# A planned attention and gMLP kernel: PSUM lent between two uses, score blocks of three, the product of the g rows moved, and a new order of tasks

## The chip, the cores and the metric

The kernel runs on one core of one Trainium2 chip. The metric is the time of one execution on the device, in microseconds (us). A core has four engines that matter here, each with its own instruction queue: TensorE (PE, the matrix multiplier; its weight loads are listed apart as PEld), ScalarE (ACT), VectorE (DVE) and GpSimd (POOL). SyncE (SP) issues transfers. Matrix products land in PSUM, which has 8 banks; one bank holds 512 float32 numbers in each of 128 partitions, and only ACT and DVE read it out here.

## The reference

Batch B = 8, heads H = 12, sequence S = 448, head width D = 64. Everything the kernel takes and gives is float32.

```python
def rmsnorm(x, g):
    return x / np.sqrt(np.mean(x * x, axis=-1, keepdims=True) + 1e-06) * g
q_n, k_n = rmsnorm(q, g_q), rmsnorm(k, g_k)
scores = q_n @ k_n^T / sqrt(64)                      # (8, 12, 448, 448)
attn = softmax(scores)                               # exp, divided by its sum
x = (attn @ v)  -> reshaped to (8, 448, 768)
h = relu(x @ w_in);  u, v = h[..., :512], h[..., 512:]
v_n = (v - mean(v)) / sqrt(var(v) + 1e-06)           # over the 512 columns
v_s = w_spatial @ v_n + b_spatial                    # mixes the 448 rows
out = (u * v_s) @ w_out                              # (8, 448, 768)
```

## The kernel before

The 96 heads are worked through in 24 groups G of four heads (three groups a batch). Of each group, in order: load q and k; square, sum over the 64 columns, take 1/rms with a logarithm and an exponential; scale q and k to bf16; turn them (by PE in the first six groups, by a transposing transfer later); seven *rounds* of scores, each of four 64-by-64 matmuls into a pair of PSUM banks, and one exponential on ACT that reads that pair; the row sums; the values (`attn @ v`); and the division. After three groups a batch is complete, and its second half follows: the units v, u, s and o, which are full 128-by-128 matmuls.

The program is not written in order. A planner holds a list of tasks, each with a cost on every engine that may do it and a position; it simulates the engines with these costs and emits the tasks in the order in which its simulation starts them. A table of nudges, found by search, shifts single tasks in it. PSUM is kept in two pools:

```python
    P_sc = Pool(many(2, [128, 2, 512], FP, "pss", psp))                 # two pairs of banks: scores
    P_w = Pool(many(4, [128, 512], FP, "ps", psp), ordered=False)       # four banks: all other matmuls
# ... cut ...
    g_t = add("g2", {"DVE": (0.3, 0.3)}, -90.0, emit, after=6.2)        # g_q * g_k / sqrt(D), one row
    # the matmul that turns the row into a column, and the copy out of PSUM: position -90.0 too
# ... cut: the first group's squares, on ACT alone ...
                if G == 0:
                    costs = {"ACT": costs["ACT"]}
# ... cut: 1/rms of a group, one task of two instructions (lines 469 and 470) ...
            act.activation(out=P_ln[G % 4], in_=ms.t, func=AF.Ln, bias=eps, scale=1.0 / D)
            act.activation(out=P_rs[G % 4], in_=P_ln[G % 4], func=AF.Exp, bias=0.0, scale=-0.5)
# ... cut: one round of scores (line 550) ...
        for h in range(2):
            for a in range(2):
                pe.matmul(out=ps[64 * h:64 * h + 64, a, 0:S], lhsT=kb[64 * a:64 * a + 64, slot, ...],
                          rhs=qb[64 * a:64 * a + 64, :, ...], start=True, stop=True)
    rounds = [(G, r) for G in range(NGT) for r in range(7)]             # 168 rounds
    blocks = [[x] for x in rounds[:21]] + [rounds[i:i + 2] for i in range(21, len(rounds), 2)]
    # a block is one task of PE: all its rounds, each into its own pair; then one exp per round (line 573)
# ... cut: sums (line 597) and values (line 618), 128 rows by 32 columns, four side by side ...
            act.activation(out=rc.t, in_=bf.t[:, 0:S], func=AF.Ln, bias=0.0, scale=1.0)     # line 605
            act.activation(out=rc.t, in_=rc.t, func=AF.Exp, bias=0.0, scale=-1.0)           # line 606
# ... cut: unit v, line 660 (six matmuls of 512 columns; its last rows line 664), unit u, line 713
#     (six of 448 columns), unit s, line 729 (four of 448), unit o, line 753 (four of 384) and 774;
#     each of these groups of matmuls fills one bank of P_w, which ACT or DVE then reads out ...
```

PE also runs matmuls of no use (line 320) on a bank set apart until 26 us[...].

Of the kernel before, what the change touches and what calls it, by code (L numbers as in the profile page):

```python
# [17 lines left out]
class Pool:  # L18


    def __init__(self, slots, ordered=True):
        self.slots = slots
        self.free = [0.0] * len(slots)
        self.ordered = ordered
        self.made = 0
        self.taken = 0

# [37 lines left out]
class Planner:  # L65
# [46 lines left out]

    def start_of(self, t, e):
# [6 lines left out]
        if t.get:  # L120
            need = {}
            for b in t.get:
                n = need.get(b.pool, 0)
                if b.pool.ordered and b.seq != b.pool.taken + n:
                    return None
                need[b.pool] = n + 1
            for p, n in need.items():
                f = sorted(p.free)[:n]
                if f[-1] == math.inf:
                    return None  # L130
                at = max(at, max(x - 0.19 * i for i, x in enumerate(f)))
        return at

    def run(self, fill=None, log=None):
# [4 lines left out]
        for t in self.tasks:  # L139
# [4 lines left out]
            if not t.deps:  # L144
                for e in t.costs:
                    cand[e].append(t)
        for _ in range(len(self.tasks)):
# [32 lines left out]
            for b in t.get:  # L180
                p = b.pool
                b.slot = min(range(len(p.slots)), key=lambda i: p.free[i])
                p.free[b.slot] = math.inf
                p.taken += 1
            n = len(self.tc.nc.cur_bb.bb.instructions) if self.tc else 0
            t.emit(e)
# [13 lines left out]
            for b in t.use:  # L200
                b.left -= 1
                b.end = max(b.end, t.done)
                if b.left == 0:
                    b.pool.free[b.slot] = b.end
# [21 lines left out]
def kernel(  # L226
# [32 lines left out]
    P_sc = Pool(many(2, [128, 2, 512], FP, "pss", psp))  # L259
    P_w = Pool(many(4, [128, 512], FP, "ps", psp), ordered=False)  # L260
# [55 lines left out]
    P_w.free[3] = 26.0  # L316

    def dummies(n):
        for _ in range(n):
            pe.matmul(out=P_w.slots[3][:, 0:128], lhsT=ident, rhs=ident, start=True, stop=True)  # L320
# [15 lines left out]
    for G in range(NGT):  # L336
        b, g = divmod(G, NG)
        for i in range(2):
# [5 lines left out]
            raw_t[G, i] = [add(f"load{i} G{G}", {"SP": (0.6, 0)}, due(G) - 26 + i * 0.1, emit, get=[bf], dma=1.4,  # L344
# [8 lines left out]
    g_t = add("g2", {"DVE": (0.3, 0.3)}, -90.0, emit, after=6.2)  # L353
# [4 lines left out]
    g_t = add("g2 col", {"PE": (0.1, 0.4)}, -90.0, emit, deps=[g_t], get=[g_b], mode="G")  # L358
# [3 lines left out]
    g_t = add("g2 copy", {"DVE": (0.1, 0.2)}, -90.0, emit, deps=[g_t], use=[g_b])  # L362
# [65 lines left out]
    for G in range(NGT):  # L428
# [11 lines left out]
        for i in range(2):  # L440
            sqb = Buf(P_sq)
            for j, h in enumerate(halves):
# [11 lines left out]
                if G == 0:  # L454
                    costs = {"ACT": costs["ACT"]}
# [12 lines left out]
        def emit(e, G=G, ms=ms_b):  # L468
            act.activation(out=P_ln[G % 4], in_=ms.t, func=AF.Ln, bias=eps, scale=1.0 / D)
            act.activation(out=P_rs[G % 4], in_=P_ln[G % 4], func=AF.Exp, bias=0.0, scale=-0.5)  # L470
        rs = add(f"rstd G{G}", {"ACT": (0.49, 0.75)}, d - (6 if early else 15), emit, deps=red[0] + red[1], use=[ms_b])
# [84 lines left out]
    blocks = [[x] for x in rounds[:21]] + [rounds[i:i + 2] for i in range(21, len(rounds), 2)]  # L556
# [22 lines left out]
    for G in range(NGT):  # L579
# [10 lines left out]
        sm = None  # L590
# [13 lines left out]
        def emit(e, bf=bf, rc=rc):  # L604
            act.activation(out=rc.t, in_=bf.t[:, 0:S], func=AF.Ln, bias=0.0, scale=1.0)
            act.activation(out=rc.t, in_=rc.t, func=AF.Exp, bias=0.0, scale=-1.0)  # L606
        rec = add(f"recip G{G}", {"ACT": (1.06, 1.19)}, pos - 2, emit, deps=[sm], get=[rc], use=[bf])
# [31 lines left out]
    for b in range(B):  # L639
# [12 lines left out]
        for c in (3, 0, 1, 2):  # L652
# [30 lines left out]
            def emit(e, c=c, n=n, vs=vs, mv=mv, b=b):  # L683
                s6 = s6s[c]
                dve.bn_stats(out=s6[0:n], in_=vs.t[0:n, c, :])  # L685
                dve.bn_aggr(out=mv.t[0:n, c, :], in_=s6[0:n])
            st.append(add(f"stats{c} b{b}", {"DVE": (0.83, 0.92)}, pos + 0.5, emit, deps=[a],
# [3 lines left out]
        def emit(e, mv=mv, rv=rv):  # L691
            act.activation(out=rv.t[:, 0, :], in_=mv.t[:, :, 1], func=AF.Ln, bias=eps, scale=1.0)
            act.activation(out=rv.t[:, 1, :], in_=rv.t[:, 0, :], func=AF.Exp, bias=0.0, scale=-0.5)
        lr = add(f"ln_rstd b{b}", {"ACT": (0.5, 0.65)}, pos, emit, deps=st, get=[rv], use=[mv])
# [98 lines left out]
    "unit_o00 b5": 2, "unit_v1 b3 0": 0.3, "relu_u1 b1": 10, "unit_u1 b6": 11, "turn0 G3 0": -16,  # L793
    "square1 G7 0 @POOL": -8, "exp G0 r2": 6, "unit_o01 b6": -11, "relu_v0 b2 @DVE": -1, "sums G17 0": 1,
    "values0 G14 0": 2, "unit_u3 b2": 21, "rstd G20": 9, "unit_o01 b7": -7, "unit_o01 b1": -3,
    "relu_u3 b2 @ACT": -5, "scaled0 G6 0 @POOL": -2, "scores [(12, 3), (12, 4)]": 2, "unit_o11 b6": -7,
    "osb00 b2 @DVE": -0.4, "exp G4 r2": 12, "unit_o20 b0": -8, "unit_s1 b5": -6, "sums G15 0": -11,
    "square0 G2 0 @POOL": -1, "unit_u0 b5": 6, "osb10 b0 @ACT": -3, "reduce0 G1 0": 5,
    "k_scale G15 @DVE": -4, "relu_v0 b2": 10, "relu_u3 b4 @ACT": 1, "unit_s0 b4": 0.4, "osb20 b6": 4,
    "unit_v3 b0 0": 1, "k_scale G10 @DVE": 3, "exp G22 r4": 17, "unit_o11 b1": 15, "osb3 b0 @DVE": 1,  # L800
    "exp G3 r3": -4, "turned1 G2 0": 52, "values0 G2 1": 6, "relu_u0 b4": -3, "unit_u3 b3": 4,
    "gate3 b0": -19, "square0 G6 0": 65, "relu_v3 b3 @ACT": -4, "load1 G17": -12, "unit_s3 b6": 6,
    "reduce1 G4 0": 6, "scores [(2, 0)]": -33, "k_scale G19 @ACT": 3, "sums G14 0": 8, "load1 G10": -3,
    "turned0 G4 0 @DVE": 7, "values1 G8 0": 18, "osb00 b0 @ACT": 4, "turn0 G4 0": 36, "gate3 b2": -23,
    "unit_u0 b3": 9, "turned0 G0 0 @DVE": 7, "scores [(15, 2), (15, 3)]": -1, "square1 G4 0 @DVE": 3,
    "square0 G4 0 @POOL": 1, "scaled0 G4 0": 45, "values0 G1 1": -27, "values1 G2 1": 6, "values1 G15 0": 6,
    "recip G1": -3, "scores [(2, 6)]": -49, "values0 G5 0": 21, "unit_o20 b7": 1.3, "exp G11 r4": 13,
    "scores [(23, 4), (23, 5)]": -20, "exp G21 r1": 13, "exp G6 r6": -13, "unit_s2 b4": -2.1,
    "square1 G6 0 @ACT": 3, "scaled1 G5 0 @DVE": 5, "square0 G1 0 @POOL": 2, "gate1 b2": -17,
    "relu_v2 b3": 11, "rstd G13": 4, "xt0 G3": 13, "unit_o3 b3": 10, "unit_v3 b3 0": 2.8, "exp G11 r5": 4,  # L810
    "k_scale G7 @DVE": -2, "unit_s2 b0": -15, "values1 G3 0": -13, "square0 G8 0": 16, "osb21 b1": -8,
    "unit_u1 b5": 23, "relu_v1 b4 @DVE": -1, "unit_u0 b1": 4, "osb00 b5 @ACT": 15, "values0 G2 0": 4,
    "osb21 b1 @DVE": -1, "unit_u1 b1": 3, "osb11 b0": 11, "load0 G2": 2, "xt1 G22": 12, "k_scale G15": 18,
    "unit_u2 b1": 2, "relu_v2 b1 @DVE": 2, "turned1 G5 0 @DVE": 16, "stats2 b2": 7.5, "sums G18 0": -7,
    "relu_v2 b0 @ACT": -1, "unit_o20 b5": 2.6, "scores [(23, 6)]": -4, "relu_v2 b4": 2, "sums G8 0": 15,
    "v b3 #4": 25, "turned0 G4 0": 12, "turned0 G5 0": 84, "reduce0 G5 0": -3, "relu_v1 b4": -5,
    "turned0 G3 0 @DVE": 4, "stats0 b0": 15, "values1 G20 0": 2, "osb00 b2": 31, "values1 G14 0": 1,
    "unit_v1 b0 4": -2, "sums G2 0": -21, "unit_s1 b2": 6, "values0 G15 0": 6,
    "scores [(14, 3), (14, 4)]": -9, "values0 G23 0": 9, "values0 G22 0": 18, "unit_u2 b6": 5,
    "osb00 b1 @ACT": -2, "scaled0 G9 0": 9, "rstd G19": 5, "w_spT1": -18, "values0 G3 0": 7,  # L820
    "scaled1 G4 0 @DVE": 7, "exp G12 r5": -3, "osb3 b0": 20, "square1 G3 0 @POOL": 12, "w_out": -13,
    "unit_u3 b1": -6, "osb21 b0 @ACT": 7, "stats0 b3": 36, "v b6 #2": 25, "reduce0 G3 0": -2,
    "values1 G23 0": 13, "unit_s1 b6": 9, "osb11 b5 @DVE": -8, "scaled1 G7 0": -14, "unit_o11 b0": 4,
    "relu_u2 b4": 10, "unit_u2 b2": 5, "relu_v3 b4 @ACT": -4, "exp G12 r4": -11, "relu_v0 b4 @ACT": -10,
    "unit_o21 b0": 3, "values0 G21 0": 12, "xt0 G19": 23, "relu_v1 b3 @DVE": -4, "exp G22 r5": 15,
    "relu_v1 b5 @ACT": 4, "values1 G22 0": 15, "k_scale G17 @ACT": -3, "values1 G0 0": 11, "exp G4 r3": 8,
    "osb20 b0 @ACT": -1, "turned1 G4 0 @ACT": -7, "recip G6": 10, "load0 G14": -7, "unit_o10 b1": 1,
    "turn0 G5 0": 66, "sums G4 0": 45, "unit_o3 b4": -22, "exp G19 r0": -3, "reduce1 G10 0": 10,
    "w_spT2": -54, "scaled1 G2 0": 4, "ln_apply0 b5": 7, "values0 G20 0": 3, "gate1 b0": -18,
    "relu_v0 b3": 12, "relu_v3 b0 @DVE": -2, "scaled1 G6 0 @POOL": -4, "exp G11 r2": 4, "ln_apply2 b1": 4,  # L830
    "sums G16 0": -7, "unit_o20 b3": -12, "xt0 G0": 16, "v b7 #2": 16, "unit_v3 b4 0": -10, "unit_u3 b6": -3,
# [43 lines left out]
```

## Time and profile before

| | |
|---|---|
| time, median of 3 runs | 284.07 us (283.93 to 284.42) |
| span of the profiled run | 282.2 us, granted PE clock 0.994 |
| DMA moved | 50.01 MB, mean 177 GB/s |
| exponentials of the scores (ACT) | 168 of 913 ns: 144.8 us |
| sums of squares (DVE) | 50 of 1039 ns: 51.0 us |
| score matmuls (PE) | 672, four at a time: 51.7 us |

How to read it: "busy" is the time in which an engine ran at least one instruction. The chain of waits follows the end of the program back, at each step to what released it; what stands in it set the time. PE's matmuls overlap, so a PE that is busy throughout is not at its peak. In the views, `pss` is a pair of banks for scores, `ps` a bank for other matmuls, `ms` the sums of squares, `lnms` and `rs` their logarithm and 1/rms, `et` the exponentials, `rc` the reciprocal of the row sums, `vt` the values, `g_row` and `g_col` the product of the g rows as a row and as a column.

### The profile page before, as it was taken

The numbers are of one execution on the slowest core, as the hardware profiler recorded it, in microseconds if no ns is written. First come the engines' busy times: TensorE is split into PE (matmuls) and PEld (weight loads), VectorE is DVE, ScalarE is ACT, GpSimd is POOL, SyncE is SP. The second block draws the span as 40 slices with busy tenths as digits, with TensorE's granted clock in tenths as the row PEclk, the third lists the DMA queues.
The fourth block names the chain that finished last, engine by engine and source line by source line (L and its number), as shares of the span: only waits on it lengthen the run. The fifth ranks groups of instructions, "written<-read, shape, count | busy, mean of one in ns | idle before, by whom it ended". The sixth has DMA issues, their size and how long they took to land.

```text
span 282.2 us, 7121 instructions
## 1 busy us (share of the span) xinstructions
PE 265.8 (94%) x2857; PEld 124.7 (44%) x2868; DVE 207.2 (73%) x348; ACT 222.7 (79%) x357; POOL 158.4 (56%) x132
## 2 busy tenths in 40 slices
PE   5788999899999999999999999999999999999990
PEld 5544455444453444444443443444444444444550
DVE  1799799987898976888787886878886757444650
ACT  4399998889977899798799889987887888773521
POOL 7563844395389767988888468985993400000011
PEclk9999999999999999999999999999999999999997
DMA  7998699298779788996999979996998280006014
GB/s 253 288 253 206 165 214 256 56 211 248 242 174 215 168 198 242 213 232 150 251 244 217 220 191 234 203 196 188 221 178 102 57 205 2 2 12 186 0 41 154
DMA packets 65378, 50.01 MB, mean 177 GB/s; under 512 B 41985, under 2 KB 61906, under 8 KB 65346
## 3 DMA queue, kind: packets, MB, share of 16 engines
q1 hardware_dynamic: 51266, 40.61, 57.1%
q0 software_dynamic: 14080, 8.96, 22.0%
q8 instruction: 22, 0.36, 0.5%
q14 instruction: 10, 0.08, 0.1%
HBM read 38.55 MB, written 11.01 MB: 176 GB/s over the span
## 4 chain that ended last, share of the span: by engine, by line
PE 81%; ACT 7%; DVE 7%; POOL 2%; issue 2%; POOLq 0%; DVEq 0%; ACTq 0%
PE pss L550 14%; PE ps L753 12%; PE ps L618 11%; PE ps L660 10%; PE ps L713 10%; PE ps L729 9%; PE ps L597 7%; ACT et L573 4%; PE ps L664 2%; PE ps L774 2%; PE ps L320 2%; DVE s L685 1%; DVE nq L483 1%; PE ps L412 1%; DVE ms L462 1%
## 5 line engine op out<-in xcount | busy, mean ns | idle before, releaser
L573 ACT ACTIVATE et<-pss 128x896 bf16<-128x896 f32 x168 | 144.8, 913 | 19.6 <-PE pss L550 19.4
L462 DVE TENSOR_REDUCE ms<-sq 128x14 f32<-128x896 f32 (+1 forms) x50 | 51.0, 1039 | 6.0 <-ACT sq L447 3.6
L550 PE MATMUL pss<-qT,kT 64*64 64x448 bf16 x672 | 51.7, 363 | 3.0 <-ACT et L573 1.6
L483 POOL TENSOR_TENSOR nk<-kf,rs 128x896 bf16<-128x896 f32 x22 | 38.0, 1730 | 16.6 <-ACT rs L470 8.0
L618 PE MATMUL ps<-et,vt 128*32 128x448 bf16 x768 | 42.8, 354 | 0.0
L627 DVE TENSOR_TENSOR xt<-ps,rc 128x448 bf16<-128x448 f32 x48 | 28.8, 621 | 17.1 <-ACT rc L606 8.8
L483 POOL TENSOR_TENSOR nq<-qf,rs 128x896 bf16<-128x896 f32 x18 | 30.4, 1692 | 17.8 <-ACT rs L470 8.0
L713 PE MATMUL ps<-xt,w_in 128*128 128x448 bf16 x192 | 40.0, 353 | 0.0
L449 POOL TENSOR_TENSOR sq<-qf 128x896 f32<-128x896 f32 x18 | 30.3, 1684 | 13.2 <-DVE kT L529 8.1
L753 PE MATMUL ps<-w_out,gt 128*128 128x384 bf16 x192 | 35.2, 327 | 0.3 <-DVE gt L734 0.3
L660 PE MATMUL ps<-w_in,xt 128*128 128x512 bf16 x133 | 33.6, 380 | 1.0 <-issue 0.6
L449 POOL TENSOR_TENSOR sq<-kf 128x896 f32<-128x896 f32 x18 | 30.3, 1682 | 3.4 <-DVE ms L462 2.8
L550 PEld LDWEIGHTS <-kT 64*64 64x64 bf16 x672 | 15.5, 104 | 34.5 <-issue 29.5
L765 POOL DMA_DIRECT2D out_dram<-osb x3 | 1.7, 557 | 48.3 <-ACT osb L741 48.3
L375 POOL DMA_DIRECT2D vt<-in_v_dram x32 | 21.6, 682 | 11.7 <-ACT qT L508 5.7
L734 DVE TENSOR_TENSOR gt<-ps,us 128x448 bf16<-128x448 f32 x32 | 19.5, 622 | 11.5 <-PE ps L729 10.1
L618 PEld LDWEIGHTS <-vt 128*32 128x32 bf16 x768 | 19.7, 96 | 18.3 <-issue 6.7
L729 PE MATMUL ps<-w_spT,vn 128*128 128x448 bf16 (+1 forms) x128 | 27.4, 354 | 0.1
L743 DVE COPY osb<-ps 128x384 f32<-128x384 f32 x35 | 18.6, 553 | 11.5 <-PE ps L753 11.1
L713 PEld LDWEIGHTS <-w_in 128*128 128x128 bf16 x192 | 17.5, 98 | 19.7 <-issue 4.9
L753 PEld LDWEIGHTS <-gt 128*128 128x128 bf16 x192 | 17.0, 98 | 16.7 <-issue 6.4
L597 PE MATMUL ps<-et,ones 128*32 128x448 bf16 x384 | 23.3, 355 | 0.3 <-DVE xt L627 0.3
(71 smaller groups left out, 286.0 us busy)
## 6 DMA issues: line engine op xcount, KB each, us to landing
qf<-in_q_dram SPq DMA_DIRECT2D x24, 448.0 KB, 4.1
kf<-in_k_dram SPq DMA_DIRECT2D x24, 448.0 KB, 5.1
out_dram<-osb SPq DMA_DIRECT2D x45, 192.0 KB, 3.3
vt<-in_v_dram POOLq DMA_DIRECT2D x16, 192.0 KB, 5.7
vt<-in_v_dram POOLq DMA_DIRECT2D x16, 144.0 KB, 5.8
w_in<-in_moe_w_in_dram POOLq DMA_DIRECT2D x2, 768.0 KB, 9.4
out_dram<-osb SPq DMA_DIRECT2D x15, 96.0 KB, 3.5
w_out<-in_moe_w_out_dram POOLq DMA_DIRECT2D x1, 768.0 KB, 9.0
```

The lines of the kernel that those rows point to most:

```text
L449: eng_of[e].tensor_tensor(out=sqb.t[:, h], in0=r.t[:, h], in1=r.t[:, h], op=ALU.mult)
L462: dve.tensor_reduce(out=ms.t[:, i, h], in_=sqb.t[:, h].rearrange("p a (s d) -> p a s d", d=D), axis=AX.X, op=ALU.add)
L483: eng_of[e].tensor_tensor(out=nb.t.rearrange("p s a d -> p a s d")[:, :, s0:s1, :], in0=r.t.rearrange("p a (s d) -> p a s d", d=D)[:, :, s ...
L550: pe.matmul(out=ps[64 * h:64 * h + 64, a, 0:S], lhsT=kb[64 * a:64 * a + 64, slot, 64 * xk:64 * xk + 64], rhs=qb[64 * a:64 * a + 64, :, 64 ...
L573: act.activation(out=eb.t[:, r], in_=bf.t[:, :, 0:S], func=AF.Exp, bias=0.0, scale=1.0)
L597: pe.matmul(out=bf.t[32 * l:32 * l + 32, 0:S], lhsT=ones[:, (0 if c < 3 else 1 + x), :], rhs=eb.t[:, r, a, :], start=(c == 0), stop=(c == ...
L618: pe.matmul(out=bf.t[32 * l:32 * l + 32, 0:S], lhsT=vb.t[:, 2 * (g + 3 * a) + x, c, half::2], rhs=eb.t[:, r, a, :], start=(c == 0), stop=( ...
L627: dve.tensor_tensor(out=xb.t[:, j * S:j * S + S], in0=bf.t[:, 0:S], in1=rc.t, op=ALU.mult)
L660: pe.matmul(out=bf.t, lhsT=xb.t[:, j * S + 128 * c:j * S + 128 * c + 128], rhs=w_in[:, j, DH:DF], start=(j == 0), stop=(j == 5))
L713: pe.matmul(out=bf.t[:, 0:S], lhsT=w_in[:, j, 128 * f:128 * f + 128], rhs=xb.t[:, j * S:j * S + S], start=(j == 0), stop=(j == 5))
L729: pe.matmul(out=bf.t[:, 0:S], lhsT=vn.t[0:kp, c, 128 * f:128 * f + 128], rhs=w_spT[0:kp, c, :], start=(c == 0), stop=(c == 3))
L753: pe.matmul(out=bf.t[:, 0:384], lhsT=gt.t[:, f, 128 * c:128 * c + 128], rhs=w_out[:, f, 384 * h:384 * h + 384], start=(f == 0), stop=(f == 3))
```

## The change

PSUM becomes one tile of 8 banks. Six of them form three pairs for scores; the other two are for other matmuls alone. Banks of the pairs are lent to other matmuls whenever the next block of scores is not ready or stands later in position. With three pairs, a block of scores from round 63 on has three rounds in place of two. The product of the g rows gets a late position, so that the first sums of squares stand ahead of it. A logarithm and the exponential behind it become two tasks, so that others can come between; so do the two steps of the mean and variance. The first group's squares may be done by DVE too. The table of nudges is searched anew for all of this. The arithmetic is the same.

```diff
+class Banks:
+    def __init__(self, pairs):
+        self.pairs = pairs
+        self.free = [0.0] * 8
+class ScorePool(Pool):                       # three pairs, in order
+    def times(self, lend):
+        f = self.banks.free
+        return [max(f[2 * i], f[2 * i + 1]) for i in range(3)]
+class BankPool(Pool):                        # eight banks; the first six only when lent
+    def times(self, lend):
+        return [x + 0.01 if i < 6 else x for i, x in enumerate(self.banks.free)] if lend else \
+            [math.inf] * 6 + self.banks.free[6:]
+    def lend(self, t):
+        s = self.scores[self.next_score] if self.next_score < len(self.scores) else None
+        return s is None or s.pos > t.pos or s.count > 0
...
-    P_sc = Pool(many(2, [128, 2, 512], FP, "pss", psp))
-    P_w = Pool(many(4, [128, 512], FP, "ps", psp), ordered=False)
+    ps = psp.tile([128, 8, 512], FP, name="ps")
+    banks = Banks([ps[:, 2 * i:2 * i + 2, :] for i in range(4)])
+    P_sc, P_w = ScorePool(banks), BankPool(banks)
...
-    g_t = add("g2", {"DVE": (0.3, 0.3)}, -90.0, emit, after=6.2)
+    g_t = add("g2", {"DVE": (0.3, 0.3)}, 5.0, emit, after=7.0)
...          (the matmul and the copy of the g row: -90.0 to 5.0 too)
                 if G == 0:
-                    costs = {"ACT": costs["ACT"]}
+                    del costs["POOL"]
...
             act.activation(out=P_ln[G % 4], in_=ms.t, func=AF.Ln, bias=eps, scale=1.0 / D)
+        rs = add(f"rstd_ln G{G}", {"ACT": (0.13, 0.35)}, ...)
+        def emit(e, G=G):
             act.activation(out=P_rs[G % 4], in_=P_ln[G % 4], func=AF.Exp, bias=0.0, scale=-0.5)
-        rs = add(f"rstd G{G}", {"ACT": (0.49, 0.75)}, ...)
+        rs = add(f"rstd G{G}", {"ACT": (0.13, 0.39)}, ..., deps=[rs], ...)
...          (the same cut in two: recip_ln and recip, ln_ln and ln_rstd, stats and aggr)
-    blocks = [[x] for x in rounds[:21]] + [rounds[i:i + 2] for i in range(21, len(rounds), 2)]
+    blocks = [[x] for x in rounds[:21]] + [rounds[i:i + 2] for i in range(21, 63, 2)] + \
+        [rounds[i:i + 3] for i in range(63, len(rounds), 3)]
...
-NUDGE = { ... "unit_u1 b1": 3, "unit_u2 b2": 5, "unit_u3 b1": -6, ... }
+NUDGE = { ... "unit_u1 b1": 463, "unit_u2 b2": 403, "unit_u3 b1": 315, ... }
```

## The prediction

> **What bounds the kernel now.** I read the page first, for the shares of the engines; then the table by stage, because an average over 282 us hides that the opening and the steady part have different limits; then the chain of waits, stage by stage.
>
> ```profile
> PE 265.8 (94%) x2857; PEld 124.7 (44%) x2868; DVE 207.2 (73%) x348; ACT 222.7 (79%) x357; POOL 158.4 (56%) x132
> ```
>
> ```profile
> 0.00:13.50 13.50, 8.71 (x89) 7.65 (x89) 6.18 (x20) 6.14 (x10) 8.77 (x22) 1.00 1.01 264
> 13.50:40.00 26.50, 23.97 (x340) 13.17 (x341) 23.61 (x30) 24.47 (x36) 16.38 (x14) 1.00 0.85 213
> 40.00:275.00 235.00, 232.49 (x2430) 103.75 (x2438) 177.38 (x300) 191.29 (x310) 132.23 (x96) 1.00 0.79 169
> ```
>
> The columns are the stretch, its length, then the busy time of PE, PEld, DVE, ACT and POOL, the clock, the DMA share and GB/s. Up to 13.5 us no score has been computed (PE's 8.71 us are mostly the matmuls of no use). From 13.5 to 40 ACT is busy 24.47 of 26.50. From 40 to 275 PE is busy 232.49 of 235.00 and ACT only 191.29: there PE is the bound, and only 2.5 us of it is idle. So a gain in the steady part has to make PE's own work shorter; filling gaps has 2.5 us to give.
>
> ```profile
> 115.76 1.24 PE ps L713 x6
> 117.00 0.50 PE pss L550 x8
> 117.51 2.38 PE ps L713 x12
> 119.88 0.50 PE pss L550 x8
> 120.39 1.63 PE ps L729 x8
> 122.01 0.50 PE pss L550 x8
> 122.52 0.87 PE ps L597 x16
> 123.39 1.51 PE ps L618 x32
> 124.90 0.50 PE pss L550 x8
> ...
> 262.85 4.54 PE ps L713 x24
> ```
>
> This is the chain in the steady part (start, us, engine, tile and line, matmuls). No other engine is in it. It shows a fixed cost of each change of tile shape. Unit u (L713) is followed in the last line by matmuls of its own shape: 24 take 4.54 us, 0.189 each. Where it is cut off by a block of scores, 12 take 2.38 (0.11 more than 12 x 0.189) and 6 take 1.24 (0.11 more). Sums and values agree: 16 sums followed by values of the same shape and 32 values behind them take 0.87 + 1.51 = 2.38 for 48 matmuls, four at a time. The block of two rounds takes 0.50, where a round inside a run takes 0.19 in rows of this chain not shown: 0.12 more. So I take 0.11 to 0.12 us for each unbroken run of one shape. Counted in PE's timeline there are 193 such runs from 40 to 275 us, hence some 22 us of the 235.
>
> ```profile
> 4.93 0.62 DVE L462 TENSOR_REDUCE ms<-sq 128x7 f32<-128x448 f32 x1 [3.58 <-ACT sq L447]
> 5.52 1.04 ACT L447 ACTIVATE sq<-kf 128x448 f32<-128x448 f32 x2 [0.15 <-DMA kf<-in_k_dram]
> ...
> 6.91 0.28 DVE L350 SCALAR_TENSOR_TENSOR g_row<-g_row 1x128 f32<-1x128 f32 x1 [1.35 <-DMA g_row<-in_g_k_dram]
> ...
> 7.91 0.16 DVE L361 COPY g_col<-ps 128x1 f32<-128x1 f32 x1 [0.72 <-PE ps L357]
> 7.98 1.66 DVE L462 TENSOR_REDUCE ms<-sq 128x7 f32<-128x448 f32 x3
> 9.68 0.32 ACT L469 ACTIVATE lnms<-ms,eps 128x28 f32<-128x28 f32 x1 [3.12 <-DVE ms L462]
> ```
>
> This is the timeline of the start. DVE finishes the first of four sums at 5.55, then stands 1.35 us for the g rows to land and 0.72 us for the matmul that turns them. All four squares are done by 6.56. Three sums that could have run wait for the g path, and the logarithm waits for them (3.12 us).
>
> ```profile
> ACT et L573 <- PE pss L550: 19.4, 38, 1.8
> ```
>
> ACT waits 19.4 us in 38 places for scores (total, times, longest): a block starts only when its pairs have been read, and ACT is idle meanwhile.
>
> **What the Trainium skill says.** "TensorEngine Tiling (Array Packing)", Key Properties: changing the tiling mode drains TensorE. The trace agrees: 0.11 us a change, and none between matmuls of one shape. "Perfetto Trace Analysis", Identifying the Most-Contended Engine: busy time of the matmuls does not tell how near PE is to its peak. That is so here: the drains above count as busy, so 99% busy still leaves something to take. The same page, Matmuls: independent groups should rotate through PSUM banks so that one is read out while the next is filled. The before kernel does it with four; its PE hardly ever waits for a reader. "PSUM — Partial Sum Buffer", PSUM bank collisions raise a hardware error: engines must be kept apart by bank, so the next writer of a lent bank waits for whichever engine read it last. The trace of before, where no bank is shared between scores and other work, shows no such wait.
>
> **The change part by part.**
>
> *g rows.* The sums can now run 4.93 to about 7.3 (four of 0.6; the last square ends at 6.56, so the last sum ends about 7.2). The logarithm follows at 7.3 in place of 9.68: 2.35 us earlier. The g product is still needed before the first turned k: DVE's 0.28 us fits while ACT does logarithm and exponential (0.32 + 0.23), the copy (0.16) falls among the scalings. Net 2.2 us at the first score (13.49 to about 11.3). What follows is ACT's row of exponentials, which moves along, unless loads or the second group's squares (on ACT at 10.16 to 11.93, now in the way of the first exponential) hold it up. I keep 1.8.
>
> *Blocks of three.* Rounds 63 to 167 are 105: 53 blocks before, 35 after, 18 fewer. Of the 54 runs of scores after 100 us, 32 stand between two runs of the same shape, so taking one away joins them and saves two runs; the other 22 save one. That is 1.59 runs a block: 18 x 1.59 x 0.11 = 3.2 us, all on PE and on the path.
>
> *Banks.* From 100 to 256 us there are 108 rounds, 1.44 us each, so a block of three every 4.33 us. Of that PE spends 3 x 0.19 + 0.11 = 0.68 on scores; in the other 3.65 it fills about three banks (1.1 us a group). A bank is held some 1.9 us (1.14 to fill, 0.6 to read, a little wait), values longer, as they wait for the reciprocal (0.55 + 0.58 on ACT). The mean need is 3.2 x 1.9 / 4.33 = 1.4 banks. Two banks cover the mean, not the peaks; the lent ones must. The exponentials follow each other at 0.83, so the last pair is free some 3 us after a block starts. I put down 1.0 us of new waits of PE.
>
> *Logs and exps apart.* ACT is not the bound in the steady part. In before it stood idle 2.1 us in all ahead of the second instruction of the 1/rms pair. Off the path: 0.2 us at most, in the opening. The same for the two steps of mean and variance on DVE.
>
> *Searched anew.* This cannot be worked out from the profile. The nudges push every unit u far back (up to 463), which makes them filler for moments when nothing else can start. The idle time of PE (2.5 us in the steady part) and the opening, where ACT stands 2 us of 26.5, bound what an order alone can give without fewer runs. I take 2.0 us: some of the idle, and a few more runs joined.
>
> Sum: -1.8 - 3.2 + 1.0 - 0.2 - 2.0 = -6.2; 284.07 - 6.2 = 277.9. I say **277.8 us**.
>
> **The rivals.** (1) *PE waits for banks.* Two fixed banks in place of four: if the planner's costs are off by a few tenths, PE stands at each lent bank, and all that is queued behind stands with it. With 0.15 us at each of 35 blocks and at some units this gives back 5 us: 282 to 284. For it speaks that DVE and ACT are at 75 to 82% in the steady part, so reading out is often late; against it the mean need of 1.4 banks. (2) *The start is hidden.* If the loads of the second and third groups or ACT's row decide the opening, the 2.2 us at the first score are gone by 40 us: 279.5. DMA share 1.01 up to 13.5 us speaks for it, the 24.47 of 26.50 of ACT against: a chain that begins earlier ends earlier. (3) *The order is the larger part.* With three pairs ACT waits less often for scores, values come sooner, and the search joins many more runs: 20 more runs gone are 2.2 us, and the opening tightens by 2: 273.5. (4) *The tail stays.* Behind 258 us there is only unit work of the last batch, in one row; nothing in the change shortens it.
>
> **Range and chances.** From 273.5 (rival 3) to 282.5 (rival 1 with the start kept). Two per cent is 5.7 us, so the line is 278.4, just above my number. The start and the drains alone make 5.0 if nothing is lost; the search was made for this layout, so a loss over 2% needs something that the planner does not see. Faster by over 2%: 0.58; within 2%: 0.37; slower: 0.05.
>
> **What would show it.** In the changed profile: the first logarithm near 7.3 us and the first score near 11.3; in the steady part some 30 fewer runs of one shape (about 165 from 40 to 275), each still 0.11; score runs of 12 matmuls of about 0.68; ACT's wait for scores under 19.4 us; PE's waits for readers of its banks about 1 us and not 5; the chain from 40 us on still PE. Wrong would be: PE idle over 5 us behind 40 us, the start of the unit v's of batch 0 (33 us) unmoved in spite of an earlier first score, or a count of runs that hardly falls.

## The result, and the profile after

The changed kernel takes 276.87 us (median of 4 runs, 276.38 to 277.71) beside 284.0 us of the kernel before: a ratio of 0.975, with a 95% interval of 0.9722 to 0.9778. It is 7.1 us faster. 277.8 us had been predicted.

The page of the changed kernel gives these shares of the engines, and its table by stage (stretch, length, busy PE, PEld, DVE, ACT, POOL, clock, DMA share, GB/s) these rows:

```profile
PE 261.5 (95%) x2859; PEld 126.7 (46%) x2859; DVE 201.3 (73%) x350; ACT 216.5 (79%) x353; POOL 160.7 (58%) x134
```

```profile
0.00:13.50 13.50, 8.78 (x92) 7.43 (x93) 7.75 (x22) 6.72 (x11) 9.13 (x22) 1.00 1.01 263
13.50:40.00 26.50, 24.55 (x355) 13.69 (x354) 22.86 (x30) 25.31 (x40) 16.91 (x15) 0.94 0.88 220
40.00:268.00 228.00, 227.41 (x2413) 105.35 (x2410) 170.66 (x300) 183.47 (x302) 133.51 (x96) 1.00 0.83 173
268.00:275.20 7.20, 0.75 (x5) 0.23 (x3) 0.04 (x1) 0.98 (x2) 1.20 (x3) 0.69 0.49 159
```

The shares hardly move: 95% in place of 94% for PE. The stages tell more. PE's last matmul ends at 268.75 us, where it ended at 275.58, and from there to the end it is 6.5 us (6.6 before), so the gain lies ahead of it. In the steady part PE is idle 0.6 us. In the profile of before it was 2.5, but 11 of the 144 unit v matmuls of 512 columns are missing from that profile, so some of its idle time is not idle. The profile of the same order with PSUM as one tile (experiment 8) has all 144, and there PE is idle 1.6 us:

```profile
40.00:275.00 235.00, 233.43 (x2440) 103.74 (x2438) 177.28 (x300) 191.28 (x310) 132.03 (x96) 1.00 0.79 169
```

The chain of waits of the changed kernel in the steady part (start, us, engine, tile and line, matmuls):

```profile
122.22 0.86 PE ps L792 x4
123.09 0.69 PE ps L604 x12
123.78 2.06 PE ps L816 x12
125.83 0.87 PE ps L652 x16
126.70 0.76 PE ps L816 x4
127.46 0.69 PE ps L604 x12
128.15 0.87 PE ps L676 x16
129.02 1.41 PE ps L816 x8
```

The blocks of scores are now L604: 12 matmuls, three rounds, in 0.69 us, against 0.50 for two before. Three rounds at 0.19 and one fixed cost of 0.12 make that. The cost of a change of shape has not changed; there are fewer changes. Counted in PE's timeline from 40 us on, runs of one shape fell from 193 to 157 (in the whole program from 237 to 195); runs of scores alone from 72 to 53.

The timeline of the start of the changed kernel:

```profile
4.96 2.34 DVE L513 TENSOR_REDUCE ms<-sq 128x7 f32<-128x448 f32 x4
...
7.22 0.27 DVE L401 SCALAR_TENSOR_TENSOR g_row<-g_row 1x128 f32<-1x128 f32 x1
7.34 0.32 ACT L520 ACTIVATE lnms<-ms,eps 128x28 f32<-128x28 f32 x1 [0.75 <-DVE ms L513]
7.69 0.23 ACT L524 ACTIVATE rs<-lnms 128x28 f32<-128x28 f32 x1
8.13 0.29 PEld L408 LDWEIGHTS ps<-one_f,g_row 1*128 1x128 f32 x2
...
8.55 0.16 DVE L412 COPY g_col<-ps 128x1 f32<-128x1 f32 x1 [1.05 <-PE ps L408]
8.62 1.16 DVE L537 TENSOR_TENSOR nk<-kf,rs 128x512 bf16<-128x512 f32 x2
...
12.04 0.76 PE L604 MATMUL ps<-qT,kT 64*64 64x448 bf16 x12 [0.61 <-DVE qT L564]
12.95 0.91 ACT L628 ACTIVATE et<-ps 128x896 bf16<-128x896 f32 x1
```

The four sums run in one row and the first logarithm stands at 7.34 instead of 9.68. But 0.7 us are given back: 1/rms is there at 7.92, and the first scaling begins at 8.62, because the copy of the g column stands ahead of it on DVE and waits for PE, which is still in its matmuls of no use until 8.13. The first exponential comes at 12.95, 1.3 us earlier than before.

### The profile page after: what moved, and what is told of

It is laid out like the page before. It is cut to its first block, busy times and chain, and to the rows that moved or that the text cites. A ratio compares the mean times of both kernels' runs of the same rounds, so it can differ in the third digit from the quotient of the medians.

```text
span 275.2 us, 7127 instructions
## 1 busy us (share of the span) xinstructions
PE 261.5 (95%) x2859; PEld 126.7 (46%) x2859; DVE 201.3 (73%) x350; ACT 216.5 (79%) x353; POOL 160.7 (58%) x134
## 4 chain that ended last, share of the span: by engine, by line
PE 64%; issue 21%; ACT 6%; POOL 5%; DVE 3%; POOLq 0%
PE ps L604 11%; PE ps L676 10%; PE ps L776 10%; PE ps L718 9%; PE ps L816 6%; PE ps L792 6%; PE ps L652 6%; ACT et L628 4%; PE ps L371 2%; POOL nk L537 2%; POOL sq L500 2%; PE ps L722 2%; PE ps L837 1%; PE ps L463 1%; DVE vn L764 1%
## 5 line engine op out<-in xcount | busy, mean ns | idle before, releaser
L628 ACT ACTIVATE et<-ps 128x896 bf16<-128x896 f32 x168 | 144.9, 917 | 21.4 <-PE ps L604 20.8
L604 PE MATMUL ps<-qT,kT 64*64 64x448 bf16 x672 | 47.4, 363 | 2.9 <-ACT et L628 2.1
L685 DVE TENSOR_TENSOR xt<-ps,rc 128x448 bf16<-128x448 f32 x48 | 28.4, 620 | 20.7 <-ACT rc L664 13.2
L500 POOL TENSOR_TENSOR sq<-kf 128x896 f32<-128x896 f32 x23 | 38.6, 1680 | 6.3 <-DVE nk L537 3.1
L676 PE MATMUL ps<-et,vt 128*32 128x448 bf16 x768 | 42.0, 354 | 0.0
L500 POOL TENSOR_TENSOR sq<-qf 128x896 f32<-128x896 f32 x19 | 32.0, 1684 | 15.0 <-issue 5.0
L537 POOL TENSOR_TENSOR nk<-kf,rs 128x896 bf16<-128x896 f32 x18 | 30.4, 1691 | 8.9 <-ACT rs L524 6.2
L816 PE MATMUL ps<-w_out,gt 128*128 128x384 bf16 x192 | 34.2, 327 | 0.2 <-DVE gt L797 0.2
L718 PE MATMUL ps<-w_in,xt 128*128 128x512 bf16 x144 | 34.2, 380 | 0.1
L604 PEld LDWEIGHTS <-kT 64*64 64x64 bf16 x672 | 16.3, 105 | 28.5 <-issue 24.5
L792 PE MATMUL ps<-w_spT,vn 128*128 128x448 bf16 (+1 forms) x128 | 27.0, 353 | 0.1
L776 PEld LDWEIGHTS <-w_in 128*128 128x128 bf16 x192 | 17.2, 98 | 20.8 <-issue 6.6
L816 PEld LDWEIGHTS <-gt 128*128 128x128 bf16 x192 | 17.5, 98 | 15.9 <-issue 4.9
L742 DVE BATCH_NORM_STATS2 s<-vs 128x6 f32<-128x512 bf16 (+1 forms) x32 | 21.6, 685 | 4.0 <-ACT vs L693 3.6
```

The source lines that it names most:

```text
L500: eng_of[e].tensor_tensor(out=sqb.t[:, h], in0=r.t[:, h], in1=r.t[:, h], op=ALU.mult)
L537: eng_of[e].tensor_tensor(out=nb.t.rearrange("p s a d -> p a s d")[:, :, s0:s1, :], in0=r.t.rearrange("p a (s d) -> p a s d", d=D)[:, :, s ...
L628: act.activation(out=eb.t[:, r], in_=bf.t[:, :, 0:S], func=AF.Exp, bias=0.0, scale=1.0)
L676: pe.matmul(out=bf.t[32 * l:32 * l + 32, 0:S], lhsT=vb.t[:, 2 * (g + 3 * a) + x, c, half::2], rhs=eb.t[:, r, a, :], start=(c == 0), stop=( ...
L685: dve.tensor_tensor(out=xb.t[:, j * S:j * S + S], in0=bf.t[:, 0:S], in1=rc.t, op=ALU.mult)
L718: pe.matmul(out=bf.t, lhsT=xb.t[:, j * S + 128 * c:j * S + 128 * c + 128], rhs=w_in[:, j, DH:DF], start=(j == 0), stop=(j == 5))
```

## The experiments

**Theory A**: the time in the steady part is PE's own work plus a fixed cost for each run of one shape; the change takes runs away and starts earlier. **Theory B**: what counts is that no wait falls on PE; runs matter little, and the search, not the block size, gave the time. **Theory C**: the earlier start is hidden by loads or by ACT's row of exponentials.

Experiments 1 to 5 and 8 keep the planner's order on every engine and move one thing by hand; a new plan would have changed everything at once. Experiments 6, 7 and 9 are planned anew.

**1. The start alone, in the kernel before.** Only the g product, its matmul and its copy move behind the four sums; 22 matmuls of no use behind it are left out.

```diff
   dve.tensor_reduce(out=ms.t[:, i, h], ...)
+  if (G, i, j) == (0, 1, 1):          # behind the fourth sum; no longer at the planned place
+      g_mul(e); g_turn(e); g_copy(e)
```

> The kernel before with its order of tasks kept on every engine; only the product of the g rows, its matmul and its copy stand behind the four first sums instead of behind the first one, and 22 matmuls of no use behind it are left out so that PE is free in time. Theory A (an earlier start is worth what it saves): first logarithm at 7.3 instead of 9.68 us, first score about 2 us earlier, and 284.0 falls by 1.3 to 2.2, to 281.8 to 282.7. Rival (the start is hidden by loads or by the row of ACT up to 40 us): first score earlier all the same, time within 0.5 of 284.0.

Measured: 282.86 us, ratio 0.9955 (0.9937 to 0.9972), so 1.1 us less. The first logarithm is at 7.99 (the loads came some 0.15 us later in this run, and DVE waits 0.55 us for a square). The timeline of this kernel, and the first exponential of the kernel before in the second fence:

```profile
7.99 0.32 ACT L475 ACTIVATE lnms<-ms,eps 128x28 f32<-128x28 f32 x1 [1.27 <-DVE ms L464]
...
12.78 0.92 ACT L579 ACTIVATE et<-pss 128x896 bf16<-128x896 f32 x1 [1.58 <-PE pss L556]
```

```profile
14.24 1.73 ACT L573 ACTIVATE et<-pss 128x896 bf16<-128x896 f32 x2 [1.76 <-PE pss L550]
```

The first exponential is 1.46 us earlier than before (12.78 against 14.24), the eighth too (20.80 against 22.26), and the last matmul of PE 1.5 us (274.07 against 275.58). The start is handed through the whole program. C falls. The amount is 1.5 us in the trace and 1.1 in the time, the latter just under A's 1.3 to 2.2.

**2. The start undone, in the changed kernel.** The same three instructions go back behind the first sum, with 38 matmuls of no use ahead and 22 behind.

```diff
   dve.tensor_reduce(out=ms.t[:, i, h], ...)
+  if (G, i, j) == (0, 0, 0):          # behind the first sum, as in the kernel before
+      g_mul(e); dummies(38); g_turn(e); g_copy(e)
```

> The changed kernel with its order kept; the product of the g rows, its matmul and its copy stand behind the first of the four sums, as in the kernel before (38 matmuls of no use ahead of that matmul, 22 behind it). Theory A: first logarithm back at about 9.7 us, and the time rises by 1.3 to 2.2 from 276.9, to 278.2 to 279.1. Rival (start hidden): 276.4 to 277.4.

Measured: 278.47 us, ratio 0.9801 (0.9764 to 0.9838), 1.6 us more than the changed kernel in its first comparison and 1.3 more than in its second (277.17, experiment 5); in this comparison the changed kernel did not run. The timeline of this kernel:

```profile
9.68 0.32 ACT L527 ACTIVATE lnms<-ms,eps 128x28 f32<-128x28 f32 x1 [3.04 <-DVE ms L515]
...
14.61 0.91 ACT L635 ACTIVATE et<-ps 128x896 bf16<-128x896 f32 x1
```

In the profile of the changed kernel from experiment 5, which had the same clock, the first exponential came at 12.74, the eighth at 20.20 and PE's last matmul ended at 268.18. Here they come at 14.61, 22.07 and 270.05: each 1.9 us later. In both orders the g path is worth between 1 and 2 us.

**3. More runs, all else the same.** Of each block of three, the third round is issued behind PE's next task. The matmuls, banks and exponentials are the same; PE has 255 runs instead of 195.

```diff
-            for (G, r), bf in zip(blk, bufs):
-                round_mm(bf.t, G, r)
+            for n, ((G, r), bf) in enumerate(zip(blk, bufs)):
+                if n < 2:
+                    round_mm(bf.t, G, r)
+                else:
+                    apart.append(((G, r), bf))      # issued behind PE's next task of another shape
```

> The changed kernel, all other instructions in the same order; of each of the 35 blocks of three rounds the third round is issued behind PE's next task, so that PE's matmuls fall into 255 unbroken runs of one tile shape instead of 195, with the same matmuls, banks and exponentials. Theory A (each run costs 0.11 to 0.13 us on the path): 60 x 0.11 to 0.13 = 6.6 to 7.8 us more, 283.5 to 284.7. Rival (what counts is when banks and exponentials come, not the number of runs; drains lie in slack): under 2.5 us more, below 279.4.

Measured: 284.66 us, ratio 1.0031 (1.0009 to 1.0053): 7.8 us more than the changed kernel in its first comparison and 7.5 more than in its second, in the upper half of A's range. Its chain of waits, over the same work as above:

```profile
124.30 0.50 PE ps L606 x8
124.80 0.88 PE ps L832 x4
125.68 0.31 PE ps L606 x4
125.99 1.41 PE ps L832 x8
127.40 0.87 PE ps L668 x16
128.27 0.76 PE ps L832 x4
129.02 0.50 PE ps L606 x8
```

A row of 12 matmuls of unit o took 2.06; cut in two by a single round it takes 0.88 + 1.41 = 2.29, and the scores 0.50 + 0.31 = 0.81 instead of 0.69. The cut costs 0.23 + 0.12 for two more runs, here more than the mean: 7.5 to 7.8 us over 60 runs are 0.12 to 0.13 us each, and PE's last matmul came 7.35 us later, 0.12 each. B's "under 2.5 us" falls. New waits do not explain it: PE is idle 1.6 us from 40 us on, 1.0 more than in the changed kernel, and nine matmuls of unit v are missing from this profile. This is the direct measure of the price: no work was added, and the kernel lost what the whole change had brought.

**4. A better start?** The copy of the g column goes behind the scalings of k, and 38 instead of 47 matmuls of no use stand ahead of its matmul.

```diff
   dve.tensor_reduce(out=ms.t[:, i, h], ...)
+  if (G, i, j) == (0, 1, 1):          # behind the fourth sum
+      g_mul(e); dummies(38); g_turn(e)
...
   eng_of[e].tensor_tensor(out=nb.t..., in1=P_rs[G % 4]..., op=ALU.mult)
+  if (G, i, n) == (0, 1, 1):          # behind the second scaling of k
+      g_copy(e)
```

> The changed kernel with its order kept; ahead of the matmul that turns the g row stand 38 matmuls of no use instead of 47, and the copy of the g column stands behind the two scalings of k instead of ahead of them. In the changed kernel the first scaling stands 0.7 us behind the end of the 1/rms (7.92 to 8.62) for that copy. Theory A: scaling at about 7.95, first exponential 0.5 to 0.7 us earlier, time 276.2 to 276.5. Rival (ACT's squares of the second group set the first exponential): the first exponential stays at 12.9 or moves by under 0.3, time 276.6 to 277.2.

Measured: 276.82 us, ratio 0.9739 (0.9693 to 0.9785): no difference from the changed kernel. The timeline of ACT shows why:

```profile
10.63 0.95 ACT L500 ACTIVATE sq<-qf 128x896 f32<-128x896 f32 x1
...
12.19 0.95 ACT L500 ACTIVATE sq<-qf 128x896 f32<-128x896 f32 x1 [0.60 <-DMA qf<-in_q_dram]
...
13.04 1.71 ACT L636 ACTIVATE et<-ps 128x896 bf16<-128x896 f32 x2
```

The first score did come earlier (11.47 against 12.04), but ahead of the first exponential ACT has the square of the third group's q in its queue, and that waits 0.60 us for its load. The rival was right in kind, though it had named the second group's squares: what was gained at 8 us is lost at 12.

**5. That square behind the first exponential** (with the late copy of 4). Beside it in the same comparison ran the changed kernel unaltered.

```diff
+  if e == "ACT" and (G, i) == (2, 0):
+      behind.append(square)            # issued behind the first exponential
```

> The changed kernel unaltered, as the measure for the three kernels beside it: 276.4 to 277.4, both theories.

> The kernel with the late copy of the g column, and in addition ACT's square of the third group's q, which waited for its load ahead of the first exponential, stands behind that exponential; all else in the same order. If the load stood in the way of the earlier start: first exponential at about 11.9 instead of 13.0 us, ACT's idle 0.6 us gone, time 0.3 to 0.7 below the changed kernel beside it. If ACT's row as a whole sets the opening: the first exponential moves, the eighth (20.7 us) does not, and the time stays within 0.3.

Measured: 277.17 us for the changed kernel (ratio 0.9766, 0.973 to 0.9802) and 276.99 us for this one (0.9755, 0.9727 to 0.9782). The first exponential of this one:

```profile
12.21 0.92 ACT L639 ACTIVATE et<-ps 128x896 bf16<-128x896 f32 x1 [0.52 <-PE ps L615]
```

It came 0.5 us earlier than in the profile of the changed kernel beside it (12.74), but the time is the same within 0.3. So an earlier first exponential alone brings nothing; in experiments 1 and 2 the eighth moved with it. That ACT's row as a whole sets the opening (25.52 us busy of 26.50 in the changed kernel) fits this, but is not shown: the eighth exponential, which would tell, came at 21.84 us, later than the changed kernel's, in a profile with a low clock (see the end).

**6. Without the search.** Both kernels with an empty table of nudges, and the changed one with blocks of two to the end.

```diff
-NUDGE = { ... }
+NUDGE = {}
# for the third kernel also:
-    ... + [rounds[i:i + 2] for i in range(21, 63, 2)] + [rounds[i:i + 3] for i in range(63, len(rounds), 3)]
+    ... + [rounds[i:i + 2] for i in range(21, len(rounds), 2)]
```

> The kernel before with an empty table of nudges: the planner's own order, 223 unbroken runs of one tile shape on PE instead of 237. Theory A (time follows the runs alone): 14 x 0.12 less than 284.0, 282.3. Theory B (the search gave mainly that PE never waits; runs count on top of that): slower than 284.0, 286 to 291, with over 5 us of idle PE from 40 us on.

> The changed kernel with an empty table of nudges: blocks of three, lent banks, the late g product and the split tasks in the planner's own order; 185 runs, 10 fewer than with the table. Theory A: 275.7. Theory B: the structure without its search is little faster than the kernel before without its own, 283 to 291, and the idle time of PE from 40 us on is what the runs save.

> As the changed kernel with an empty table, but with blocks of two to the end: 216 runs instead of 185. Theory A: 31 x 0.12 = 3.7 us slower than the run with blocks of three and an empty table. Theory B (a block of three takes six banks at once; without a search PE stands for banks more than the 31 runs save): the same or faster than the blocks of three, with less idle PE.

| kernel | runs | time, us | ratio (95%) |
|---|---|---|---|
| before, empty table | 223 | 288.09 | 1.014 (1.0117 to 1.0162) |
| after, empty table, blocks of three | 185 | 285.01 | 1.0038 (1.0023 to 1.0053) |
| after, empty table, blocks of two | 216 | 283.99 | 0.9996 (0.9979 to 1.0012) |

Without a search the structure is worth 3.1 us, and its blocks of three are 1.0 us *slower* than its blocks of two, with 31 fewer runs. A in its plain form, time by the number of runs, falls here; the times that B expected came true for all three kernels (of its idle PE of over 5 us in the first, 3.0 came). 31 runs at 0.12 to 0.13 save about 3.9 us, so some 4.9 us must come back. The waits of PE in the kernel with blocks of three and an empty table (us in total, times, longest) and a stretch of PE's timeline (the first of these waits lies in the opening):

```profile
PE ps L408 <- DVE g_row L401: 2.9, 1, 2.9
PE ps L604 <- ACT et L628: 2.5, 7, 1.0
PE ps L652 <- ACT et L628: 1.4, 3, 0.7
PE ps L604 <- ACT kT L581: 1.3, 1, 1.3
PE ps L792 <- DVE vn L764: 1.0, 1, 1.0
```

```profile
182.11 0.57 PE L604 MATMUL ps<-qT,kT 64*64 64x448 bf16 x8
183.94 0.38 PE L604 MATMUL ps<-qT,kT 64*64 64x448 bf16 x4 [1.26 <-ACT kT L581]
184.26 0.93 PE L792 MATMUL ps<-w_spT,vn 128*128 128x448 bf16 x4
```

Here a block of three reaches from one group into the next: two rounds of the old group run, and the third stands 1.26 us in the middle of the block for the turned k of the new group, with unit s behind it. PE's idle time hides short waits, since a matmul's record lasts some 0.36 us while the next one starts 0.19 behind it. So such gaps were counted in PE's timeline from 40 us on, where a run took over 0.25 us beyond its matmuls at the rate of their columns. They hold 7.4 us beyond the usual 0.13 with blocks of three and 3.3 us with blocks of two. That is 4.1 of the 4.9 us. In the searched kernel they hold 1.9 us. So a block of three saves on the path only when the order sees to it that all it needs is there.

The search took 8.1 us off the changed kernel (285.0 to 276.9), and the old search 4.1 off the old one (288.1 to 284.0). The 8.1 us are not fewer runs: the search adds ten (185 to 195). They are 5.5 us of gaps closed and 2.5 us in the opening, where the first exponential comes at 12.95 us instead of 15.43. Without the search PE stands 2.9 us in the opening for the product of the g rows, whose instruction takes 0.27 us in the searched kernel and 3.29 here:

```profile
7.32 3.29 DVE L401 SCALAR_TENSOR_TENSOR g_row<-g_row 1x128 f32<-1x128 f32 x1
```

Why it takes so long here is not shown. Also open: no kernel with lent banks and blocks of two was searched, so how much of the whole gain needs the third round is not measured.

**7. Without lending** (and an empty table): while scores are left, all other matmuls have two banks.

```diff
-        return s is None or s.pos > t.pos or s.count > 0
+        return s is None
```

> The changed kernel with an empty table and without lending: while scores are left, all other matmuls have their two banks alone; 178 runs (185 with lending). If two banks cover the need, as the mean of 1.4 banks in the prediction would have it: 284 to 286, as with lending (285.0). If the lent banks carry it: 293 or more, with PE's waits for DVE and ACT as readers of these two banks above 8 us.

Measured: 297.86 us, ratio 1.0495 (1.0451 to 1.0539), 12.9 us more than with lending, with 7 fewer runs. The waits of PE in this kernel:

```profile
PE ps L816 <- DVE xt L685: 3.3, 6, 1.1
...
PE ps L792 <- DVE xt L685: 2.1, 4, 1.0
```

Units s and o (L792, L816) stand for DVE's division of values (L685), which has nothing to do with their operands: it is the last reader of the bank that they are to fill. All waits for readers of PSUM banks outside the scores sum to 9 to 10 us, and the gaps, counted as in experiment 6, rise from 7.4 to 20.8 us. The lent banks carry the layout, as far as kernels without a search show it; the searched kernel was not run without lending.

**8. One tile of PSUM** in the kernel before, with its pools otherwise as they were.

```diff
-    P_sc = Pool(many(2, [128, 2, 512], FP, "pss", psp))
-    P_w = Pool(many(4, [128, 512], FP, "ps", psp), ordered=False)
+    ps = psp.tile([128, 8, 512], FP, name="ps")
+    P_sc = Pool([ps[:, 2 * i:2 * i + 2, :] for i in range(2)])
+    P_w = Pool([ps[:, 4 + i, :] for i in range(4)], ordered=False)
```

> The kernel before, order and table kept; only PSUM is cut from one tile of 8 banks (two pairs for scores, four single banks) instead of six tiles. Both theories: no difference, 283.7 to 284.3. If one tile brings waits of its own (a bank held longer because the whole tile counts), 285 or more, and the changed kernel would gain by going back.

Measured: 283.88 us, ratio 0.9995 (0.9985 to 1.0005). One tile costs nothing and gives nothing; it is only the means to lend.

**9. Fewer runs still.** The changed kernel with its table searched on, with a charge on each change of shape: 186 runs.

```diff
-NUDGE = { ... "unit_u1 b1": 463, ... }
+NUDGE = { ... found from the above, 186 runs instead of 195 ... }
```

> The changed kernel with a table of nudges searched on from its own, with a charge on every change of tile shape: 186 unbroken runs instead of 195, the same structure. Theory A: 9 x 0.12 = 1.1 us below the changed kernel beside it, 275.5 to 276.1, if no waits come with the new order. Rival (what the search gains is only timing): within 0.4 of it.

Measured: 276.04 us, ratio 0.9722 (0.969 to 0.9753), beside 277.17 of the changed kernel in the same comparison: 1.1 us less, as much as 9 runs at 0.12. The intervals of the two ratios overlap, so this difference alone is no proof; the traces agree with it (PE's last matmul at 267.12 against 268.18 us). But only 5 of the 9 runs are gone from 40 us on, which makes 0.6 us; another 0.5 are gaps, counted as in experiment 6 (1.9 to 1.4 us). So this run fits A without testing it alone. It is the fastest version here. Its table by stage up to PE's last matmul, against the changed kernel's in the next fence:

```profile
40.00:267.10 227.10, 226.71 (x2411) 104.72 (x2409) 171.59 (x304) 182.37 (x298) 133.61 (x96) 1.00 0.82 174
```

```profile
40.00:268.20 228.20, 227.60 (x2411) 105.37 (x2409) 170.14 (x299) 183.32 (x303) 134.11 (x97) 1.00 0.83 173
```

PE is idle 0.4 and 0.6 us in them. Little is left to fill; fewer runs or less work would have to shorten this part.

## Why the prediction was right, and where it was not

**The total.** -6.2 us were worked out and 7.1 measured. The two causes that were worked out from the trace, the later g product and the price of a run, were each shown by runs of their own. The 7.1 us close as follows: 1.1 to 1.9 for the start (experiments 1 and 2, by time and by trace), 36 runs fewer from 40 us on at 0.12 to 0.13, so 4.3 to 4.7 (experiment 3), and PE's idle time in the steady part, 1.6 to 0.6 us. That is 6.4 to 7.6. That the number came so near is in part luck: 1.0 us of waits was charged that did not come, while the runs and the search were put too low.

**The start** was put at 1.8 and is 1.1 to 1.6 by the time, 1.5 to 1.9 by the traces. The first logarithm was right (7.3 said, 7.34 seen), the first score was not (11.3 said, 12.04 seen). The step that failed is "the copy falls among the scalings": it stands ahead of them and holds them 0.7 us. Experiments 4 and 5 show that mending this alone brings nothing.

**The blocks** were put at 18 fewer with 1.59 runs each at 0.11, so 28.6 runs. 19 runs of scores are gone from the steady part, 36 of all shapes, and the price is 0.12 to 0.13. With empty tables the blocks of three alone take 31 runs away. What the step left out is its condition. As an edit alone, blocks of three gain nothing (experiment 6).

**The banks** were put at +1.0 for new waits of PE. In the searched kernel waits did not grow, they shrank (PE idle 1.6 to 0.6 us); in the kernel with an empty table blocks of three bring about 4 us. The mean need of 1.4 banks is of little use: with two banks alone the time rises by 12.9 us. The need goes over two banks often enough to matter, and the lending meets that. A loss of the size of rival 1 (282 to 284) came only without a search (285.0). That the kernel before shows no wait for the reader of a bank of the other matmuls was not quite right: its sums wait once, 0.3 us, for DVE's division (`PE ps L597 <- DVE xt L627: 0.3, 1, 0.3`).

**The search** is the term that was mis-sized. -2.0 was a guess from the idle time that was left. Against what the old search had given, the new one gives 4.0 us more (8.1 and 4.1), and the structure without a search 3.1, where the other terms of the prediction sum to 4.2. The reason was another too: not "a few more runs joined", since the search adds runs, but gaps closed and an earlier opening (experiment 6). Rival 3, that the order is the larger part, was right in the size, 4.0 of 7.1, and not in its reason, many more runs joined. And not every unit u is pushed back, but 29 of 32.

**Logs and exps apart** (-0.2) were not tried alone.

**Signs that failed.** ACT's wait for scores was to fall below 19.4 us; it is 20.8 us in 31 places:

```profile
ACT et L628 <- PE ps L604: 20.8, 31, 2.1
```

Most of it is off the path: in experiment 9 it is 13.8 us, and the time only 1.1 us less. The first unit v was to move forward from 33 us; it went back to 38.3. A single task's place is no measure of progress once the order is searched. The chain "still PE" holds for the stretch shown, but between 56 and 72 us it runs over POOL, ACT and DVE too, and the page of the changed kernel puts 21% to "issue": its last store hangs on POOL, whose work before that lies 44 us back, and the chain loses its way there.

## What to carry to other kernels

When an engine is busy 99%, count what its busy time is made of: here 157 changes of tile shape at 0.12 to 0.13 us are some 20 us of 228, and making the unit between two changes longer was one lever. A longer unit needs more of everything at once, operands and banks, so try it together with the order of tasks and with buffers that can be lent. When testing one part of a planned kernel, hold the plan and move that one thing; an edit that plans anew measures the plan.

## What the hardware showed that was not expected

The granted clock of PE in the opening differs between executions of the same order. In the result's profile of the changed kernel it was half of full speed for one stretch, which makes the 0.94 in the second row of its table:

```profile
14.80:18.10 3.30, 3.26 (x27) 1.75 (x27) 3.30 (x4) 3.03 (x6) 1.87 (x3) 0.50 1.10 258
```

In the profile of the same kernel from experiment 5 it was full from 13.5 to 40 us:

```profile
13.50:40.00 26.50, 23.91 (x357) 13.37 (x357) 23.22 (x31) 25.52 (x40) 16.68 (x15) 1.00 0.91 224
```

With the half stretch the eighth exponential began at 20.74 us, without it at 20.20; 0.2 of these 0.5 us were there at the first exponential already (12.95 against 12.74). In the kernel of experiment 5 with the square moved the clock was half from 10.8 to 20.9 us, and the eighth exponential began at 21.84; that execution took 278.57 us, where the median of its kernel is 276.99. The matmuls of no use were 84 in both profiles of the changed kernel, so their number does not decide it. Of its four runs in the first comparison the two with a mean clock of 0.996 and 0.997 took 276.6 and 276.4 us, the two with 0.986 and 0.987 took 277.2 and 277.7. Why one execution is granted more than another is not shown.
